# One more pair of half-products in a fused attention and feed-forward kernel, and a new order of its instructions

## The chip, the cores and the metric

The kernel runs on one core of a Trainium2 chip. The metric is the device time of one execution in microseconds (us). Besides the core's engines TensorE (PE; its weight loads are PEld), VectorE (DVE), ScalarE (ACT) and GpSimd (POOL), the queue of SyncE (SP) issues the transfers (DMA).

## The reference

Three stages follow each other, with B = 2 sequences of 448 tokens, 12 heads of 64 and a model width of 768:

```python
attn = softmax(where(causal, q @ k.T / 8, -1e9)) @ v          # per head
x = attn as [896 tokens, 768]
h = maximum(maximum(x @ w1, x @ w2), x @ w3)                  # 768 x 768 each
y = h @ w_out                                                 # 768 x 768
g = where(z > 0, z, exp(minimum(z, 0)) - 1), z = y @ w_in     # 768 x 2048
out = g @ w_out2                                              # 2048 x 768
```

All of it is in float32.

## The kernel before, in words

**Products.** A matrix product of float32 accuracy is made of three matmuls: both factors are split into a high and a low part in the type fp32r, and hi*hi, hi*lo and lo*hi are summed in PSUM. A block is one 128-column block f of a weight matrix, for both sequences; its moving operand is 128 x 448. `standard` makes one block of ph (x times w1, w2 or w3; n = 0, 1, 2) with 2 x 6 x 3 = 36 matmuls of 448 columns. `unit` makes two blocks at once in the manner of Strassen: seven half-products of 9 matmuls each, 63 in all, where two standard blocks need 72. Its operands are the two blocks' weights and differences of them (f13, f24), and, of x, sums that are made once for all units (`sums_x`).

**Weights.** A weight block comes by DMA as raw int64 and goes through `load_steps`: three short DVE steps (L184, L187, L189), one ACT step (L191), one DVE step (L193); then ACT makes hi (L211, L727 in a unit) and DVE makes lo (L199). A unit adds one difference of full width and two halves (L744) and takes four splits to hi and lo instead of two. What a block's matmuls leave in PSUM goes to SBUF through ACT for n = 0 (L233) and is joined by DVE with a maximum for n = 1 and 2 (L235); in a unit two of the four outputs first get the shared term s5 added by DVE (L628). During a unit ACT copies the running sum from one PSUM bank to another three times (L799) and s5 once (L813).

**Stages.** The attention of 12 head pairs comes first (until 93.3 us on PE); scores `s`, transposes `pt` of the probabilities and outputs `o` alternate there, and 54 matmuls of early ph blocks fill gaps. ACT or DVE copies a transposed bank from PSUM to SBUF (`th<-pt`, L271) before PE may reuse it; there are two banks. Then come ph, py = h times w_out, pg (with the exp) and po, where three pairs of pg and two of po are units too (the last is o4). In ph block 0, block 5 and, of n = 0, the blocks 1 and 2 are standard; units are made of the block pairs (1, 2) and (3, 4): 1_1, 2_1, 0_3, 1_3, 2_3 (n, first block).

**Order.** Every engine works its instructions off in the order written. That order comes from a planner, `Plan`: a list of tasks with costs per engine (ns), needs, buffers taken and given, and a rank; at each step it takes the task that can begin first, or one within `SLACK` ns of that with a smaller rank. One plan covers the attention (its ranks are `LEADS` and `SHIFTS`, and the engine of a normalise, a guard or a copy is chosen by it), one, `late_plan`, all the rest (ranks are PE's time at the task). `LAG` is the time from a task's end to its follower's start. Nothing of these numbers runs on the chip: they decide order and, where a task may go to several engines, the engine.

Of the kernel before, what the change touches and what calls it, by code (L numbers as in the profile page):

```python
# [51 lines left out]
    "exps": -18.87, "guard": -543.14, "inverse": -213.22, "keep": 263.11, "least": 284.28, "load": -700.35,  # L52
# [4 lines left out]
    "x_hi": -414.57, "x_lo": -284.77,  # L57
}
SHIFTS = {
# [10 lines left out]
class Plan:  # L70
# [9 lines left out]
    SLACK = 62  # L80
# [5 lines left out]
    SWITCHES = 100  # L86

# [5 lines left out]
    def add(self, fn, args, engines, pair, after=(), takes=(), gives=(), mode=None, lead=None):  # L93
        if lead is None:
            lead = LEADS.get(f"{fn.__name__}{args[0]}" if args else None, LEADS.get(fn.__name__))
        rank = pair + lead + self.shifts.get(len(self.tasks), 0)
        t = {"fn": fn, "args": args, "engines": engines, "pair": pair, "rank": (rank, len(self.tasks)),
             "after": [a for a in after if a], "takes": list(takes), "gives": list(gives), "mode": mode}
        self.tasks.append(t)
        return t  # L100
# [4 lines left out]
    def begins(self, t, free):  # L105
        ready = {}
        for e, cost in t["engines"].items():
            at = free[e] + (self.switch(t["mode"]) if e == "PE" else 0)
            for a in t["after"]:
                at = max(at, a["end"] + (35 * (e in self.OVER) if a["eng"] == e else self.LAG[a["eng"]]))  # L110
            for k in set(t["takes"]):
                n = t["takes"].count(k)
                if len(self.slots[k]) < n:
                    return None
                at = max(at, sorted(self.slots[k])[n - 1])
            ready[e] = at
        return min((at + t["engines"][e], at, e) for e, at in ready.items())

    def order(self, free=()):
        free = dict.fromkeys(self.LAG, 0) | dict(free)  # L120
        left, out = list(self.tasks), []
        while left:
# [8 lines left out]
            free[eng] = end - self.OVER.get(eng, 0)  # L131
            if eng == "PE":
                self.mode = t["mode"]
# [15 lines left out]
def fused_kernel(ctx: ExitStack, tc: tile.TileContext, qk, v, w1, w2, w3, wo, wi2, wo2, outT):  # L149
# [93 lines left out]
    with ExitStack() as s2:  # L243
# [58 lines left out]
        def add_totals(c, k, after=None, plan=plan, lead=20):  # L302

            t1, t2, t3, t4 = (totals[q, c] for q in range(4))
            out, a, b = ((t3, t2, t1), (t2, t1, t2), (t4, t4, t2))[k]

            def total(eng):
                nc.vector.tensor_tensor(out=out, in0=a, in1=b, op=ALU.subtract)

            need = [kept[c], kept[NPAIR + c]] if k == 0 else [after]  # L310
            return plan.add(total, (), {"DVE": 619}, 0, need, lead=NPAIR + c + THIRD if k == 0 else lead + c)

        def pair(p):
# [142 lines left out]
            def finish(s):  # L456
# [3 lines left out]
                for part in PARTS:  # L460
# [3 lines left out]
                    for i, j in sorted(mine, key=lambda ij: -ij[0]):  # L464
                        w = min(C * (i + 1), S)
                        flat[i, j] = plan.add(
                            normalise, (i, j), {"POOL": 240 + int(0.84 * w), "DVE": 100 + int(0.7 * w)}, p, [a])
# [36 lines left out]
        def weights(k):  # L504
# [8 lines left out]
            for s, (eng, cost) in enumerate((("DMA", 4200), *LOAD[1:], ("ACT", 760), ("DVE", 880))):  # L513
                t = plan.add(
                    step, (), {eng: cost}, GATES[k], [t or xs_done[GATES[k]]], takes={0: ["raw"], 1: ["f"]}.get(s, []),
                    gives={5: ["raw"], 7: ["f"]}.get(s, []))
# [32 lines left out]
        for steps in begun.values():  # L549
# [5 lines left out]
            for k, (eng, cost) in enumerate(LOAD):  # L555
                t = plan.add(
                    step, (), {eng: cost}, B * NPAIR, [t or xs_done[NPAIR + HALF + 1], xs_done[NPAIR + HALF + 2 - (k == 0)]],
                    takes=[["raw"], ["f"]][k] if k < 2 else [], gives=["raw"] * (k == len(LOAD) - 1), lead=19)
# [24 lines left out]
    late_plan.OVER = {"DVE": 60, "ACT": 60}  # L583
    late_plan.SLACK = 110
    late_plan.LAG = Plan.LAG | {"ACT": 120, "DVE": 120}
# [111 lines left out]
    def unit(name, src, lean, left, sums, leave, kind="p"):  # L697
# [74 lines left out]
        split("13", tk, "t", at + 1800, [t1, opened], slice(0, NK), [(ut, name, 2)])  # L772
        split("24", tk, "t", at + 3600, [t4, opened], slice(0, NK), [(u, name, 3)] if lean else [ut])
# [59 lines left out]
    for f in UNITS[0]:  # L833
        standard(0, f, range(B))
# [13 lines left out]
    for fs_ in UNITS:  # L848
        for n in range(1 if fs_ == UNITS[0] else 0, 3):
# [188 lines left out]
    if PO_UNITS:  # L1038
        for c in range(HALF):
            d, tot, t = c + HALF, {}, None  # L1040
            at = begin + 22000 + 6000 * c
# [23 lines left out]
    def put(f, b, ps, after, at, eng, gives, more=None, frees=()):  # L1065
# [11 lines left out]
        task(lambda eng: None, "-", 2500, at, [t], gives=["ot"])  # L1077
# [82 lines left out]
```

## Time and profile before

| | |
|---|---|
| runs, us | 474.38, 476.13, 1632.58; median 476.13 |
| profiled execution, us | 475.4, of which the span is 473.5 |
| busy: PE, DVE, ACT, POOL | 464.2, 397.7, 281.4, 46.5 us |
| granted clock of PE over the span | 0.999 |
| attention on PE | to 93.3 us |
| ph after the attention, py | 93.3 to 203.6, from 203.6 us |

The profiled execution lies 0.7 us below the median; 1.9 us of it lie outside the span. In the rows below a time is us from the start of the span; a duration behind the start is that of the instruction (a group "x2" that of both), and the number in brackets is the idle time of the engine before it, with the instruction that ended it. PE's matmuls are pipelined: one starts before the one ahead has ended, so its pace is read from starts.

### The profile page before, as it was taken

To read this page: it belongs to the slowest core of one execution; us is meant where nothing else is said; L and a number is where in the kernel's file an instruction comes from. 1 tells how busy PE (TensorE), PEld (TensorE's weight loads), DVE (VectorE), ACT (ScalarE), POOL (GpSimd) and SP (SyncE) were. 2 spreads that over 40 slices of the span, in tenths; PEclk is the share of its full clock that TensorE was granted. 3 is DMA by queue.
4 is the path that set the end of the run, shared out by engine and by line. 5 is a ranking of instruction groups with operands and counts; after the bars stand their busy time and mean duration, and the time that the engine had idled before them with its cause. 6 is when DMAs were issued, how large, how long until landed. Compare 5 with 4: busy or idle time off the path is not lost.

```text
span 473.5 us, 6942 instructions
## 1 busy us (share of the span) xinstructions
PE 464.2 (98%) x2510; PEld 408.1 (86%) x2510; DVE 397.7 (84%) x826; ACT 281.4 (59%) x574; POOL 46.5 (10%) x97
## 2 busy tenths in 40 slices
PE   8999989999999999999999999999999999999997
PEld 3665757799999999999999999999999999999896
DVE  4999998499899999899989898999879999677301
ACT  6999885492455655454645887888766435433300
POOL 3655673000000000000000000000000000000000
PEclk9999999999999999999999999999999999999999
DMA  6652422223435234323331331434343431655002
GB/s 210 213 168 112 138 74 65 93 78 124 157 117 190 70 134 135 127 82 125 134 133 68 115 122 38 143 118 133 125 122 112 141 118 63 184 173 177 13 0 78
DMA packets 13969, 55.88 MB, mean 118 GB/s; under 512 B 1520, under 2 KB 3568, under 8 KB 13936
## 3 DMA queue, kind: packets, MB, share of 16 engines
q1 hardware_dynamic: 13936, 55.45, 35.0%
q8 instruction: 19, 0.31, 0.3%
q14 instruction: 14, 0.11, 0.1%
HBM read 52.69 MB, written 2.75 MB: 117 GB/s over the span
## 4 chain that ended last, share of the span: by engine, by line
PE 80%; DVE 10%; DMA 4%; ACT 2%; POOL 2%; issue 1%; SPq 0%; DVEq 0%; ACTq 0%; POOLq 0%
PE pg L895 10%; PE p L786 8%; PE py L895 6%; PE ps L786 6%; PE po L895 5%; PE pg L899 5%; PE ph L222 4%; PE ph L224 4%; PE ph L221 4%; PE pg00g L786 3%; PE pt L386 3%; PE py L899 3%; DMA raw_wo<-in_wo 3%; PE po L899 3%; PE s L339 3%; PE o L409 2%
## 5 line engine op out<-in xcount | busy, mean ns | idle before, releaser
L895 PE MATMUL pg<-x,hi_wi 128*128 128x448 f32 x240 | 57.7, 362 | 0.0
L895 PEld LDWEIGHTS pg<-x,hi_wi 128*128 128x128 f32 x240 | 45.0, 188 | 3.0
L363 ACT ACTIVATE pr<-pr,nmx 128x384 f32<-128x384 f32 (+2 forms) x72 | 35.9, 503 | 6.3 <-DVE nmx L353 5.8
L221 PE MATMUL ph<-x,hi_w 128*128 128x448 f32 x96 | 36.2, 377 | 0.0
L222 PE MATMUL ph<-x,hi_w 128*128 128x448 f32 x96 | 35.0, 364 | 0.1
L895 PE MATMUL py<-h,hi_wo 128*128 128x448 f32 x144 | 34.6, 362 | 0.0
L376 POOL TENSOR_SCALAR pr<-pr,r 128x256 f32<-128x256 f32 (+2 forms) x62 | 32.4, 541 | 21.0 <-DVE r L372 10.7
L899 PE MATMUL pg<-x,lo_wi 128*128 128x448 f32 x120 | 33.7, 362 | 0.0
L353 DVE CUSTOM_DVE_ANT_0 pr<-s,mask 128x384 f32<-128x384 f32 (+2 forms) x72 | 26.3, 414 | 6.0 <-PE s L339 6.0
L191 ACT ACTIVATE f_wo<-f_wo,lift 128x640 uint32<-128x640 int16 (+1 forms) x20 | 17.3, 873 | 21.4 <-DVE f_wo L189 21.4
L224 PE MATMUL ph<-x,lo_w 128*128 128x448 f32 x96 | 30.0, 363 | 0.0
L895 PEld LDWEIGHTS py<-h,hi_wo 128*128 128x128 f32 x144 | 27.0, 188 | 1.8
L339 PE MATMUL s<-qk 64*128 64x384 f32 (+3 forms) x192 | 26.8, 440 | 1.6 <-DMA qk<-in_qk 1.2
L386 PE MATMUL pt<-ident,pr 128*128 128x128 f32 x144 | 22.4, 280 | 2.8 <-ACT th L271 1.9
L386 PEld LDWEIGHTS pt<-ident,pr 128*128 128x128 f32 x144 | 16.0, 140 | 9.8 <-ACT th L271 3.7
L199 DVE SCALAR_TENSOR_TENSOR lo_wo<-f_wo,hi_wo 128x640 fp32r<-128x640 f32 (+1 forms) x20 | 17.5, 874 | 7.8 <-ACT hi_wo L211 7.5
L899 PEld LDWEIGHTS pg<-x,lo_wi 128*128 128x128 f32 x120 | 22.5, 188 | 1.5
L339 PEld LDWEIGHTS s<-qk 64*128 64x128 f32 (+1 forms) x192 | 14.2, 174 | 10.5 <-DVE nmx L353 4.3
L211 ACT ACTIVATE hi_wo<-f_wo 128x640 fp32r<-128x640 f32 (+1 forms) x20 | 15.7, 785 | 12.3 <-PE po00o L895 8.4
L409 PE MATMUL o<-th,v 128*64 128x448 f32 (+2 forms) x144 | 21.7, 439 | 0.0
L899 PE MATMUL py<-h,lo_wo 128*128 128x448 f32 x72 | 20.2, 362 | 0.0
L193 DVE SCALAR_TENSOR_TENSOR f_wo<-raw_wo,f_wo 128x640 int32<-128x640 int32 (+1 forms) x20 | 17.3, 875 | 3.2 <-ACT f_wo L191 3.1
(282 smaller groups left out, 1256.3 us busy)
## 6 DMA issues: line engine op xcount, KB each, us to landing
raw_w<-in_w SPq DMA_DIRECT2D x18, 768.0 KB, 4.4
raw_wo<-in_wo SPq DMA_DIRECT2D x12, 768.0 KB, 4.6
raw_wi<-in_wi SPq DMA_DIRECT2D x10, 768.0 KB, 4.3
raw_wo<-in_wo SPq DMA_DIRECT2D x12, 640.0 KB, 4.2
qk<-in_qk SPq DMA_DIRECT2D x11, 448.0 KB, 4.2
raw_wg<-in_wi SPq DMA_DIRECT2D x6, 768.0 KB, 4.5
v<-in_v SPq DMA_DIRECT2D x12, 256.0 KB, 2.7
out_t<-ot SPq DMA_DIRECT2D x12, 224.0 KB, 2.0
```

What stands on the lines that cost most here:

```text
L221: nc.tensor.matmul(ps, hi[:, c, :], xs[cc][:, 0, :], start=(cc == 0), stop=False)
L222: nc.tensor.matmul(ps, hi[:, c, :], xs[cc][:, 1, :], start=False, stop=False)
L224: nc.tensor.matmul(ps, lo[:, c, :], xs[cc][:, 0, :], start=False, stop=(cc == total - 1))
L339: nc.tensor.matmul(out, us[e]["qk"][own, 0, C * i:w], us[e]["qk"][own, 1, :w], start=True, stop=True, skip_group_check=True)
L353: nc.vector.tensor_tensor_reduce(out=pr, in0=u["s", g][j or 0][:, at:at + w], in1=mask_r if i == NB else mask[:, FULL - w:], scale=-0.125, ...
L363: nc.scalar.activation(pr, pr, AF.Exp, bias=u["nmx"][:, n:n + 1], scale=-1.0, accum_out=u["l"][:, n:n + 1])
L376: engines[eng].tensor_scalar(out=u["pr", j, i], in0=u["pr", j, i], scalar1=u["r"][:, n:n + 1], scalar2=1.0, op0=ALU.mult, op1=ALU.mult)
L386: nc.tensor.transpose(pt[:e - C * c, at:at + C], u["pr", j if j is None else j ^ odd, i][:, C * c:e], ident)
L409: nc.tensor.matmul(u["o"][D * j:D * (j + 1), C * c:], u["v"][:, j, c], u["th_r"][:, j ^ odd] if c == NB else u["th"][:, c, j ^ odd, C * c: ...
L786: nc.tensor.matmul(ps[0], wt[:, HALF * kk + c], w[:, i, :], start=(new and c == m == 0), stop=(c == HALF - 1 and m == 2), skip_group_check ...
L895: nc.tensor.matmul(p[0], hi[:, c, :], xs[j][c0 + c][:, i, :], start=first and c == 0 and i == 0, stop=False, skip_group_check=True)
L899: nc.tensor.matmul(p[0], lo[:, c, :], xs[j][c0 + c][:, 0, :], start=False, stop=last and c == n - 1, skip_group_check=True)
```

## The change

It does four things. The blocks 1 and 2 of n = 0 become a sixth unit, 0_1, ahead of 1_1. The attention's plan knows a port that DVE and POOL share in three kinds of task, costs the steps on DVE, ACT and POOL 3% more, has a larger SLACK and new ranks; so the order within the attention is another one, and some tasks change engine. The late plan assumes that a DMA takes 1000 ns longer to be seen, and lets DVE's steps overlap by 10 ns more. In units the splits "13" and "24" are due 1.2 us earlier, and the sums for po's units are due later for c = 0 by 6 us, for c = 1 by 4 and for c = 2 by 2.

```diff
 LEADS = {
-    "exps": -18.87, "guard": -543.14, "inverse": -213.22, "keep": 263.11, "least": 284.28, "load": -700.35,
+    "exps": 52.55, "guard": -472.28, "inverse": -311.74, "keep": 224.45, "least": 404.69, "load": -635.7,
...
 SHIFTS = {
-    20: 7.26, 22: -5.68, 24: -1.5, 34: -2.97, 62: 2.91, 91: -7.56, 93: -2.32, 96: -3.16, 97: -13.83, 98: -6,
+    22: -0.83, 31: 1.23, 96: -3.49, 97: -11.46, 103: -1.13, 112: 2.49, 119: -0.88, 142: -0.54, 143: -0.44, 176: 8.48,
...
-    SLACK = 62
+    SLACK = 78
...
+    PORT = ("DVE", "POOL")
+    PACE = 1.03
...
+        engines = {e: int(c * self.PACE + 0.5) if e in ("DVE", "ACT", "POOL") else c for e, c in engines.items()}
...
+            if t["port"] and e in self.PORT:
+                at = max(at, free["port"])
...
+            if t["port"] and eng in self.PORT:
+                free["port"] = end
...
-            return plan.add(total, (), {"DVE": 619}, 0, need, lead=NPAIR + c + THIRD if k == 0 else lead + c)
+            return plan.add(
+                total, (), {"DVE": 619}, 0, need, lead=NPAIR + c + THIRD if k == 0 else lead + c, port=True)
...
-                            normalise, (i, j), {"POOL": 240 + int(0.84 * w), "DVE": 100 + int(0.7 * w)}, p, [a])
+                            normalise, (i, j), {"POOL": 240 + int(0.84 * w), "DVE": 100 + int(0.7 * w)}, p, [a], port=True)
...
-    late_plan.OVER = {"DVE": 60, "ACT": 60}
+    late_plan.OVER = {"DVE": 70, "ACT": 60}
+    late_plan.PACE = 1
     late_plan.SLACK = 110
-    late_plan.LAG = Plan.LAG | {"ACT": 120, "DVE": 120}
+    late_plan.LAG = Plan.LAG | {"ACT": 120, "DVE": 120, "DMA": 3000}
...
-        split("13", tk, "t", at + 1800, [t1, opened], slice(0, NK), [(ut, name, 2)])
-        split("24", tk, "t", at + 3600, [t4, opened], slice(0, NK), [(u, name, 3)] if lean else [ut])
+        split("13", tk, "t", at + 600, [t1, opened], slice(0, NK), [(ut, name, 2)])
+        split("24", tk, "t", at + 2400, [t4, opened], slice(0, NK), [(u, name, 3)] if lean else [ut])
...
-    for f in UNITS[0]:
-        standard(0, f, range(B))
...
-        for n in range(1 if fs_ == UNITS[0] else 0, 3):
+        for n in range(3):
...
-            at = begin + 22000 + 6000 * c
+            at = begin + 28000 + 4000 * c
...
-        task(lambda eng: None, "-", 2500, at, [t], gives=["ot"])
+        task(lambda eng: None, "DMA", 700, at, [t], gives=["ot"])
```

The changed kernel is nine lines longer, so its line numbers are 8 to 11 higher (L184 to L199 become L192 to L207, L744 becomes L755, L799 becomes L810).

First place: DVE right behind the last low part of `sums_x`. Before, two standard loads stand there (f_w0_1 and f_w0_2), with the maxima of block 5 (best0_5, best1_5) between:

```order
L184 TENSOR_SCALAR f_w0_1_1620<-raw_w0_1_1554 128x768
L187 TENSOR_SCALAR f_w0_1_1620<-f_w0_1_1620 128x768
L189 TENSOR_TENSOR f_w0_1_1620<-f_w0_1_1620 128x768
L184 TENSOR_SCALAR f_w0_2_1635<-raw_w0_2_1563 128x768
L187 TENSOR_SCALAR f_w0_2_1635<-f_w0_2_1635 128x768
L189 TENSOR_TENSOR f_w0_2_1635<-f_w0_2_1635 128x768
L193 SCALAR_TENSOR_TENSOR f_w0_1_1620<-raw_w0_1_1554,f_w0_1_1620 128x768
L235 TENSOR_TENSOR best0_5_1611<-ph1_0_5_1572,best0_5_1611 128x448
L235 TENSOR_TENSOR best1_5_1614<-ph1_1_5_1573,best1_5_1614 128x448
L199 SCALAR_TENSOR_TENSOR lo_w0_1_1681<-f_w0_1_1620,hi_w0_1_1680 128x768
L193 SCALAR_TENSOR_TENSOR f_w0_2_1635<-raw_w0_2_1563,f_w0_2_1635 128x768
L199 SCALAR_TENSOR_TENSOR lo_w0_2_1690<-f_w0_2_1635,hi_w0_2_1689 128x768
```

With the change the two blocks of unit 0_1 stand there. Ahead of the rows shown, the three short steps stand twice in both kernels, for the same two raw blocks:

```order
L201 SCALAR_TENSOR_TENSOR b_0_1_1620<-raw_w0_1_0_1554,b_0_1_1620 128x768
L243 TENSOR_TENSOR best0_5_1611<-ph1_0_5_1573,best0_5_1611 128x448
L243 TENSOR_TENSOR best1_5_1614<-ph1_1_5_1574,best1_5_1614 128x448
L201 SCALAR_TENSOR_TENSOR b_0_1_1620<-raw_w0_1_1_1563,b_0_1_1620 128x768
L755 TENSOR_TENSOR f13_0_1_1687<-b_0_1_1620 128x768
L207 SCALAR_TENSOR_TENSOR lo0_0_1_1642<-b_0_1_1620,hi0_0_1_1641 128x768
L755 TENSOR_TENSOR f24_0_1_1698<-b_0_1_1620,f13_0_1_1687 128x384
L755 TENSOR_TENSOR f24_0_1_1698<-b_0_1_1620,f24_0_1_1698 128x384
L207 SCALAR_TENSOR_TENSOR lo13_0_1_1696<-f13_0_1_1687,hi13_0_1_1695 128x768
L207 SCALAR_TENSOR_TENSOR lo1_0_1_1690<-b_0_1_1620,hi1_0_1_1689 128x384
L207 SCALAR_TENSOR_TENSOR lo24_0_1_1703<-f24_0_1_1698,hi24_0_1_1702 128x768
```

Behind the same start, DVE now has a full difference, two halves, three full lows and a half low of unit 0_1 (lo0, lo13, lo1, lo24), where there were two lows.

Second place: ACT in the attention, at the first transposes of head pair 9 (th9 from pt9_0, pt9_1, ...; pr10 and pr11 are exps of the pairs 10 and 11, x7 and t0_1 are copies of pair 7's output):

```order
L363 ACTIVATE pr11_0_2_1074,l11_1057<-pr11_0_2_1074,nmx11_1056 128x384
L363 ACTIVATE pr11_0_0_1076,l11_1057<-pr11_0_0_1076,nmx11_1056 128x128
L271 CAST x7_1119<-o7_1078 128x448
L425 COPY t0_1_81<-o7_1078 128x448
L363 ACTIVATE pr11_1_1_1117,l11_1057<-pr11_1_1_1117,nmx11_1056 128x256
L271 COPY th9_1135<-pt9_0_1125 128x384
L271 COPY th9_1135<-pt9_1_1130 128x384
L363 ACTIVATE pr11_0_1_1121,l11_1057<-pr11_0_1_1121,nmx11_1056 128x256
L271 COPY th9_1135<-pt9_3_1144 128x2x128
```

With the change:

```order
L279 CAST x7_1101<-o7_1073 128x448
L434 COPY t0_1_81<-o7_1073 128x448
L372 ACTIVATE pr11_0_2_1063,l11_1053<-pr11_0_2_1063,nmx11_1052 128x384
L372 ACTIVATE pr11_0_0_1065,l11_1053<-pr11_0_0_1065,nmx11_1052 128x128
L372 ACTIVATE pr11_1_1_1118,l11_1053<-pr11_1_1_1118,nmx11_1052 128x256
L279 COPY th9_1132<-pt9_1_1127 128x384
L372 ACTIVATE pr10_None_3_1125,l10_904<-pr10_None_3_1125,nmx10_903 128x448
```

The copy of pt9_0 has left ACT (DVE makes it now), and x7 and t0_1 stand ahead of the exps of pair 11 that they followed.

Third place: ACT in the last unit, o4 (pos0o4, pos1o4 and pos2o4 are the copies of a running sum from bank to bank, s5_o4 the shared term, f_wo2_5_11 a weight step of the last piece):

```order
L799 COPY pos0o4_4542<-po00o4_4510 128x448
L813 COPY s5_o4_4556<-po130o4_4532 128x448
L191 ACTIVATE f_wo2_5_11_4544<-f_wo2_5_11_4544,lift_69 128x640
L799 COPY pos1o4_4569<-po00o4_4510 128x448
L211 ACTIVATE hi_wo2_4_6_4581<-f_wo2_4_6_4500 128x640
L799 COPY pos2o4_4596<-po00o4_4510 128x448
```

With the change:

```order
L810 COPY pos0o4_4548<-po00o4_4516 128x448
L824 COPY s5_o4_4560<-po130o4_4538 128x448
L810 COPY pos1o4_4575<-po00o4_4516 128x448
L199 ACTIVATE f_wo2_5_11_4573<-f_wo2_5_11_4573,lift_69 128x640
L219 ACTIVATE hi_wo2_4_6_4589<-f_wo2_4_6_4509 128x640
L810 COPY pos2o4_4603<-po00o4_4516 128x448
```

The copy pos1o4 now stands ahead of the weight step f_wo2_5_11, which it followed.

## Rows read from the trace of the kernel before

**Rows 1.** The page's part 1: busy time, share, instructions.

```profile
PE 464.2 (98%) x2510; PEld 408.1 (86%) x2510; DVE 397.7 (84%) x826; ACT 281.4 (59%) x574; POOL 46.5 (10%) x97
```

**Rows 2.** Waits of PE, whole run: total us, times, longest.

```profile
PE pt L386 <- ACT th L271: 1.9, 2, 1.2
...
PE pt L386 <- DVE th L271: 0.7, 2, 0.4
PE po00o L786 <- ACT pos1o L799: 0.5, 1, 0.5
```

**Rows 3.** Windows, 100 to 200 us: busy by engine, clock.

```profile
100.00:200.00 100.00, 100.00 (x501) 93.84 (x500) 93.51 (x154) 53.59 (x83) 0.00 (x0) 1.00 0.36 125
```

**Rows 4.** Timeline, PE: start, duration, instruction, idle before.

```profile
94.60 0.36 PE L221 MATMUL ph<-x,hi_w 128*128 128x448 f32 x1
95.10 0.47 PE L222 MATMUL ph<-x,hi_w 128*128 128x448 f32 x1
...
140.60 0.56 PE L786 MATMUL p<-x,hi 128*128 128x448 f32 x2
...
191.00 0.36 PE L786 MATMUL p<-x,hi 128*128 128x448 f32 x1
...
438.60 0.36 PE L786 MATMUL pos0o<-h,lo_o 128*128 128x448 f32 x1
439.46 0.47 PE L786 MATMUL po00o<-x,hi_o 128*128 128x448 f32 x1 [0.50 <-ACT pos1o L799]
...
469.73 0.36 PE L899 MATMUL pos2o<-c,lo_wo 128*128 128x448 f32 x1
```

**Rows 5.** DVE's instructions by line and shape, 118 to 203 us.

```profile
L193 DVE SCALAR_TENSOR_TENSOR b<-raw_w,b 128x768 int32<-128x768 int32 x10 | 9.5, 954 | 1.1 <-ACT b L191 0.7
L199 DVE SCALAR_TENSOR_TENSOR lo<-f,hi 128x768 fp32r<-128x768 f32 x10 | 9.3, 952 | 0.1
...
L189 DVE TENSOR_TENSOR b<-b 128x768 int16<-128x768 int16 x10 | 5.6, 557 | 0.3
L744 DVE TENSOR_TENSOR f<-b,f 128x384 f32<-128x384 f32 x10 | 5.6, 557 | 0.3
L184 DVE TENSOR_SCALAR b<-raw_w 128x768 bf16<-128x768 bf16 x10 | 5.5, 553 | 0.0
L744 DVE TENSOR_TENSOR f<-b 128x768 f32<-128x768 f32 x5 | 4.8, 958 | 0.2
...
L187 DVE TENSOR_SCALAR b<-b 128x768 int16<-128x768 int16 x10 | 3.6, 356 | 0.2
L199 DVE SCALAR_TENSOR_TENSOR lo<-b,hi 128x384 fp32r<-128x384 f32 x5 | 2.8, 551 | 0.0
L628 DVE TENSOR_TENSOR p<-p,s 128x448 f32<-128x448 f32 x4 | 2.5, 631 | 0.2 <-ACT ps L799 0.2
```

**Rows 6.** Timeline, DVE: lo of the first and of the last unit.

```profile
130.67 0.95 DVE L199 SCALAR_TENSOR_TENSOR lo<-b,hi 128x768 fp32r<-128x768 f32 x1
...
183.68 0.95 DVE L199 SCALAR_TENSOR_TENSOR lo<-b,hi 128x768 fp32r<-128x768 f32 x1
```

**Rows 7.** Timeline, DVE and then ACT, before the wait at 439.46.

```profile
436.67 0.50 DVE L184 TENSOR_SCALAR f_wo<-raw_wo 128x640 bf16<-128x640 bf16 x1 [2.45 <-DMA raw_wo<-in_wo]
...
438.15 0.83 ACT L191 ACTIVATE f_wo<-f_wo,lift 128x640 uint32<-128x640 int16 x1 [2.21 <-DVE f_wo L189]
438.88 0.52 ACT L799 COPY pos1o<-po00o 128x448 f32<-128x448 f32 x1
```

**Rows 8.** Timeline, ACT and then PE, at pair 9's first transposes.

```profile
70.45 0.46 ACT L271 COPY th<-pt 128x384 f32<-128x384 f32 x1
...
70.96 0.44 PE L386 MATMUL pt<-ident,pr 128*128 128x128 f32 x2 [1.20 <-ACT th L271]
```

**Rows 9.** Timeline, POOL and then DVE, in pair 10's normalising.

```profile
66.64 3.52 POOL L376 TENSOR_SCALAR pr<-pr,r 128x384 f32<-128x384 f32 x6 [0.44 <-DVE r L372]
...
67.67 0.63 DVE L187 TENSOR_SCALAR f_w<-f_w 128x768 int16<-128x768 int16 x1
```

More of the change, by code (lines that the diff above doesn't have):

```diff
@@ L51 @@
 LEADS = {
-    "exps": -18.87, "guard": -543.14, "inverse": -213.22, "keep": 263.11, "least": 284.28, "load": -700.35,
[4 rows of a table removed]
-    "x_hi": -414.57, "x_lo": -284.77,
+    "exps": 52.55, "guard": -472.28, "inverse": -311.74, "keep": 224.45, "least": 404.69, "load": -635.7,
+    "load_v": 396.21, "normalise": 579.04, "product": 387.48, "scores0": 506.37, "scores1": 154.12,
[3 rows of a table added]
+    "whole": -301.71, "x_hi": -404.34, "x_lo": -415.07,
 }
 SHIFTS = {
[3 rows of a table removed]
[4 rows of a table added]
 }
@@ L91, in __init__, with add @@
         self.parts, self.tasks, self.mode = {}, [], None
-    def add(self, fn, args, engines, pair, after=(), takes=(), gives=(), mode=None, lead=None):
+    def add(self, fn, args, engines, pair, after=(), takes=(), gives=(), mode=None, lead=None, port=False):
         if lead is None:
             lead = LEADS.get(f"{fn.__name__}{args[0]}" if args else None, LEADS.get(fn.__name__))
+        engines = {e: int(c * self.PACE + 0.5) if e in ("DVE", "ACT", "POOL") else c for e, c in engines.items()}
         rank = pair + lead + self.shifts.get(len(self.tasks), 0)
         t = {"fn": fn, "args": args, "engines": engines, "pair": pair, "rank": (rank, len(self.tasks)),
-             "after": [a for a in after if a], "takes": list(takes), "gives": list(gives), "mode": mode}
+             "after": [a for a in after if a], "takes": list(takes), "gives": list(gives), "mode": mode, "port": port}
         self.tasks.append(t)
@@ L119, in order @@
     def order(self, free=()):
-        free = dict.fromkeys(self.LAG, 0) | dict(free)
+        free = dict.fromkeys((*self.LAG, "port"), 0) | dict(free)
         left, out = list(self.tasks), []
@@ L515, in weights @@
                     step, (), {eng: cost}, GATES[k], [t or xs_done[GATES[k]]], takes={0: ["raw"], 1: ["f"]}.get(s, []),
-                    gives={5: ["raw"], 7: ["f"]}.get(s, []))
+                    gives={5: ["raw"], 7: ["f"]}.get(s, []), port=True)
             return t
@@ L557, in fused_kernel @@
                     step, (), {eng: cost}, B * NPAIR, [t or xs_done[NPAIR + HALF + 1], xs_done[NPAIR + HALF + 2 - (k == 0)]],
-                    takes=[["raw"], ["f"]][k] if k < 2 else [], gives=["raw"] * (k == len(LOAD) - 1), lead=19)
+                    takes=[["raw"], ["f"]][k] if k < 2 else [], gives=["raw"] * (k == len(LOAD) - 1), lead=19,
+                    port=True)
         with tc.manual_schedule():
```

12 rows, old and new, of tables (LEADS, SHIFTS) are left out of this document.

## The prediction

> **What bounds the kernel now.** I read the page's busy times first: PE is busy for 464.2 of 473.5 us [rows 1]. Then the waits of PE: apart from waits at the start, little is left, 2.6 us on copies of transposed banks in the attention (1.9 behind ACT, 0.7 behind DVE) and one wait of 0.5 us near the end [rows 2]. Then a window of ph: from 100 to 200 us PE is busy without a gap, at a granted clock of 1.00 (the 2.4 GHz level), while DVE is at 93.5% and POOL does nothing [rows 3]. So the time is the number of matmuls times their pace, plus a few waits; and DVE is the engine that could become the next bound.
>
> The pace is read from starts. Between 140.60 and 438.60 every 448-column matmul starts 0.200 us behind the one ahead: 298.0 us are 1,490 steps of 0.200 [rows 4]. Behind the wait at 439.46 it is slower: 147 matmuls (27 of the unit, 120 of the last pieces) have 146 steps, 29.2 us at 0.200, but the last starts 30.27 us later, so 0.207 a step and 1.1 us lost. The wait at 95.10 (0.50 us from the start ahead, so 0.30 late) left no such trace, as the pace behind it shows [rows 4]. Why one wait changes the pace and another doesn't, no row says; I keep both possibilities.
>
> **PE's work.** Two standard blocks have 72 matmuls, the unit that takes their place 63. Nine fewer, at 0.200: **-1.8 us**, all on the path, since PE has no gap there.
>
> **DVE's work for it.** A standard block's load costs, by [rows 5], 553 + 356 + 557 + 954 + 952 = 3,372 ns, two of them 6.7 us. Their outputs, of n = 0, leave by ACT. The unit costs 2 x (553 + 356 + 557 + 954) = 4,840 for both raw blocks, 958 + 2 x 557 = 2,072 for the differences, 3 x 952 + 551 = 3,407 for the lows and 2 x 631 = 1,262 for adding s5: 11.6 us. DVE has 4.8 us more, and PE passes the stretch 1.8 us sooner. ACT gets some 2.4 us more (at 53.6% busy in this stretch [rows 3] it hides that); transfers are the same two blocks.
>
> What covers it is DVE's lead over PE. Before, the first unit's lo is done at 130.67 + 0.95 = 131.6 and PE starts the unit at 140.60, 9.0 us later; for the last unit it is 184.6 against 191.00, 6.4 us [rows 4, 6]. Taking 4.8 + 1.8 = 6.6 from these leaves 2.4 and -0.2 us, if none of DVE's idle time (6.5 of the 100 us [rows 3]) is won back. The first of all, 0_1, is no problem: from the last low part of the sums, near 115, DVE needs its two loads, two maxima (2 x 0.63) and one low, 7.1 us, so 122; PE comes at 140.6 - 14.4 = 126.2. The later splits of a unit (13, 24) are due earlier in DVE's order than before, which helps the half-products that use them second and third. So the worst places are the units 0_3, 1_3 and 2_3, where I expect leads near zero, and waits of PE between 0 (idle time is won back) and 1.5 us (it isn't, and a split comes after its half-product's turn). I take **+0.5**. What is late next is w_out's first block, for which DVE has the same 6.6 us less; but PE loses there only what DVE has not caught up by then, and these waits themselves give DVE its lead back.
>
> **The last unit.** In the row of ACT the copy pos1o4 stands behind a weight step that waits for DVE, which had waited 2.45 us for a transfer: landing near 436.7, DVE's steps, ACT at 438.15, the copy at 438.88, PE at 439.46 [rows 7, 4]. In the new order the copy stands first and needs only PE's own sum, done before. The weight step that now waits behind it is of a piece used 87 matmuls, some 18 us, later. So the wait goes: **-0.5**. With no wait there, the pace should stay at 0.200: **-1.1** more. The bounds of this second part are 0 (the slower pace comes from something else at the end) and 1.1; I take all, since the unit's own matmuls ran at 0.200 until the wait.
>
> **The attention.** Its work is the same, in another order; what the order can win is PE's waits, 2.6 us, and some time in switching between kinds of matmul. The longest, 1.20 us at 70.96, is for ACT's copies of pair 9's banks, which start at 70.45 behind the exps of pair 11 [rows 8]. In the new order the first of these copies has gone to DVE, so it no longer stands in that queue; the second still stands behind three exps. The other wait behind ACT, the remaining 0.7, is behind pair 10's copies, whose neighbours stand in the same order as before. I take half of the 1.2 and nothing else, about **-0.7** with the smaller ones. Bounds: -2.6 (all waits go), and +2.6 (as many new ones come: on ACT and DVE 65 to 80 instructions stand ahead of each pair's output, in another sequence, and nothing in the trace excludes a new collision).
>
> Four guards, short steps, also go from POOL to DVE, where no wait of PE hangs on them alone, and the port's model keeps weight steps and normalises apart. The row shows what there is to win: L187, 356 ns alone, took 630 ns beside a run of POOL's normalises [rows 9, 5], so 0.27 us of DVE for one instruction. The Trainium skill, "SBUF — State Buffer", section "Who interferes with whom", says that the port pair is an exclusive lock and that the one who loses "fully blocks": by that rule a step behind one normalise would wait for all of it, 3.52 / 6 = 0.59 us [rows 9]. The trace has 0.27, less than a whole one. With ten such steps the order could free at most 3 us of DVE by the row and 6 by the rule; both are DVE's, and PE gains no more of them than the 2.6 us of waits.
>
> **The sum.** 475.4 - 1.8 + 0.5 - 0.5 - 1.1 - 0.7 = **471.8 us** against the profiled execution, which lies 0.7 below the median shown.
>
> **Rivals.**
> 1. DVE becomes the bound in the last three units. For it: 93.5% busy with 4.8 us to add and 1.8 us less time makes 98.3 of 98.2 us; DVE would have to run without a gap, and 1.1 us of its gaps were waits for ACT's step inside a load [rows 3, 5]. Against: the leads start at 6 to 9 us. Then PE waits for what isn't won back, 2 to 4 us in place of 0.5: 473.3 to 475.3, the whole gain of the unit eaten. Chance 0.15.
> 2. The other side: one such wait, at 0_3 (PE near 164), changes the pace to 0.207 as the wait at 439.46 did. From there some 1,500 matmuls follow; 1,500 x 0.0073 = 11 us, and the 1.1 of the end isn't won: 471.8 + 11 = 483, slower than before. It decides from the first wait on that the pace doesn't forget. For it: 147 matmuls kept it to the end. Against: the wait at 95.10 left none, and it needs a wait first. From 0_1 on (126 us) it would be 1,690 x 0.0073 = 12 us, 484. Chance 0.11.
> 3. The attention's new order is worse: new waits of 2.6 us instead of 0.7 won, so 475.1; twice that gives 478. For it: the planner's model is not the chip. Against: the one wait that can be followed by its queue gets shorter. Chance 0.13.
> 4. The wait at the end stays or comes elsewhere in po, since the loads of the last pieces are also moved (both transfers now stand behind four outputs on SP's queue) and the sums of po's units are due later: -1.8 + 0.5 - 0.7 alone, 473.4. Chance 0.10.
> 5. The attention wins all its 2.6 and the units lose nothing: 475.4 - 1.8 - 1.6 - 2.6 = 469.4. Chance 0.12.
>
> The forecast itself, 470 to 474, has 0.39.
>
> **Range and chances.** The forecast, the rivals 1, 3, 4 and 5 lie between 469 and 478.5; left out are rival 2 and what I don't see. So 468.5 to 478.5. Two per cent, about what a measurement of this kernel can tell from no change, are 9.5 us: faster is below 466.6, slower above 485.7. No case reaches 466.6: 0.03 for what I don't see. The pace of rival 2 with rival 3's waits would pass 485.7: 0.03. Within 2%: 0.94.
>
> **What would show it.** Right: 63 matmuls in place of 72 at a pace of 0.200; PE's waits on DVE's lo in the units under 1.5 us in sum; no wait on pos1o4 and 0.200 to the end; py begins near 201 to 202 (203.6 - 1.8 + 0.5 - 0.7 = 201.6). Wrong: starts 0.207 apart behind the first wait (rival 2); waits of PE for lo of 2_3 or of w_out over 2 us (rival 1); PE leaving the attention later than 93.3 (rival 3).

## The result and the profile after

The changed kernel takes 471.38 us (median of 4 runs, 470.25 to 471.69), the kernel before in the same series 475.65: a ratio of 0.9914, 95% interval 0.9886 to 0.9942. It is a little faster, and inside the 2% called no change. The forecast was 471.8. An execution over 1.5% above the fastest of its kernel (1632.58 us of the kernel before, and one of 482.17 and one of 483.92 further down) counts in a median and not in a ratio. Without the 1632.58 the kernel before has a median of 475.17, and in the later series, to which the ratios of the experiments refer, 475.02 to 475.44.

The profiled execution took 470.25 us, its span is 468.4: 5.1 less than the 473.5 of before. That is more than the 4.3 between the medians (3.8 from 475.17), because the profiled execution of the changed kernel is the fastest of its four, 1.1 us below their median. The page's first part, answering [rows 1]:

```profile
PE 461.6 (99%) x2501; PEld 406.8 (87%) x2501; DVE 400.7 (86%) x833; ACT 287.0 (61%) x582; POOL 44.0 (9%) x93
```

Nine matmuls fewer, 3.0 us more of DVE, 5.6 more of ACT. The waits of PE (us in total, times, longest; two more at the start are left out), answering [rows 2]:

```profile
PE s L348 <- DMA qk<-in_qk: 1.4, 2, 1.0
...
PE pt L395 <- POOL pr_None L385: 0.2, 1, 0.2
PE pt L395 <- DVE th L279: 0.2, 1, 0.2
```

The reader is to see what is missing: no wait on ACT is left, in the attention or at the end, and none on a `lo` of the units. The window from 100 to 200 us, answering [rows 3] (duration of the window, then busy time of PE, PEld, DVE, ACT, POOL, the granted clock):

```profile
100.00:200.00 100.00, 100.00 (x502) 93.88 (x501) 96.71 (x160) 54.83 (x86) 0.00 (x0) 1.00 0.34 120
```

DVE went from 93.5 to 96.7 and PE still has no gap. PE's timeline at the borders of the stages (first ph behind the attention, py, po, the last matmul), answering [rows 4]:

```profile
91.75 0.47 PE L229 MATMUL ph<-x,hi_w 128*128 128x448 f32 x1
...
200.26 0.36 PE L904 MATMUL py<-h,hi_wo 128*128 128x448 f32 x1
...
353.26 0.36 PE L904 MATMUL po<-h,hi_wo 128*128 128x448 f32 x1
...
464.66 0.36 PE L908 MATMUL pos2o<-c,lo_wo 128*128 128x448 f32 x1
```

One border of the kernel before is needed beside those of its rows and its table, the start of po:

```profile
356.60 0.36 PE L895 MATMUL po<-h,hi_wo 128*128 128x448 f32 x1
```

Cut at these borders the difference falls apart into clean parts. The same cuts serve for every experiment; the first transpose (pt) separates the start, which waits for the first transfers, from the attention. The cuts are of the profiled execution, the median is of all:

| kernel | start to pt | pt to ph | ph to py | py to po | po to last | median us |
|---|---|---|---|---|---|---|
| before | 11.87 | 81.43 | 110.30 | 153.00 | 113.13 | 475.65 |
| changed | 12.65 | 79.10 | 108.51 | 153.00 | 111.40 | 471.38 |
| unit alone, first series | 12.33 | 81.35 | 109.70 | 158.10 | 115.11 | 482.01 |
| unit alone, again | 12.81 | 81.41 | 109.17 | 153.00 | 111.55 | 473.67 |
| unit and earlier splits | 12.01 | 81.37 | 108.51 | 153.00 | 111.40 | 472.22 |
| lag of a DMA alone | 14.21 | 81.43 | 110.31 | 153.00 | 111.40 | 474.76 |
| changed, no unit | 12.73 | 79.50 | 110.31 | 153.00 | 111.40 | 472.57 |
| changed, old attention | 12.32 | 81.55 | 108.51 | 153.00 | 111.40 | 472.35 |
| changed, no port | 14.27 | 81.03 | 109.13 | 153.00 | 111.40 | 473.06 |
| changed, late splits | 13.19 | 79.48 | 109.11 | 158.10 | 115.11 | 480.38 |
| changed, a wait early | 13.00 | 79.08 | 109.87 | 153.00 | 111.40 | 472.91 |
| changed, DVE late in 1_3 | 12.54 | 79.54 | 109.01 | 153.00 | 111.40 | 471.44 |
| unit alone, a wait in pg | 14.20 | 81.41 | 109.17 | 154.39 | 111.40 | 476.12 |
| changed, one more pair in pg | 12.93 | 79.08 | 108.51 | 151.90 | 113.08 | 471.61 |

The difference is +0.78 at the start, -2.33 in the attention, -1.79 in ph, 0 in py and pg, -1.73 in po: -5.07. The start differs from profile to profile (11.87 to 14.27 in these fourteen) with the landing of the first transfers; nothing is read from it. The attention takes 79.08 to 79.54 in the six profiles with the whole of the new order and 81.35 to 81.55 in the seven with the old one, so its gain is 1.8 to 2.5.

### The profile page after: what moved, and what is told of

It reads as the page before. It is cut to its first block, busy times and chain, and to the rows that moved or that the text cites. A ratio compares the mean times of both kernels' runs of the same rounds, so it can differ in the third digit from the quotient of the medians.

```text
span 468.4 us, 6919 instructions
## 1 busy us (share of the span) xinstructions
PE 461.6 (99%) x2501; PEld 406.8 (87%) x2501; DVE 400.7 (86%) x833; ACT 287.0 (61%) x582; POOL 44.0 (9%) x93
## 4 chain that ended last, share of the span: by engine, by line
PE 93%; DVE 3%; DMA 1%; POOL 1%; ACT 1%; issue 0%; SPq 0%
PE pg L904 10%; PE p L797 9%; PE ps L797 7%; PE py L904 6%; PE po L904 5%; PE pg L908 5%; PE pt L395 4%; PE s L348 4%; PE o L418 4%; PE pg00g L797 3%; PE py L908 3%; PE ph L230 3%; PE ph L232 3%; PE ph L229 3%; PE po L908 3%; PE po00o L797 2%
## 5 line engine op out<-in xcount | busy, mean ns | idle before, releaser
L385 POOL TENSOR_SCALAR pr<-pr,r 128x384 f32<-128x384 f32 (+2 forms) x62 | 32.3, 540 | 22.4 <-DVE r L381 15.5
L199 ACT ACTIVATE f_wo<-f_wo,lift 128x640 uint32<-128x640 int16 (+1 forms) x20 | 17.4, 875 | 19.0 <-DVE f_wo L197 19.0
L229 PE MATMUL ph<-x,hi_w 128*128 128x448 f32 x72 | 27.4, 381 | 0.0
L230 PE MATMUL ph<-x,hi_w 128*128 128x448 f32 x72 | 26.2, 365 | 0.1
L207 DVE SCALAR_TENSOR_TENSOR lo_wo<-f_wo,hi_wo 128x640 fp32r<-128x640 f32 (+1 forms) x20 | 17.5, 875 | 7.5 <-ACT hi_wo L219 7.2
L232 PE MATMUL ph<-x,lo_w 128*128 128x448 f32 x72 | 23.2, 363 | 0.0
L797 PE MATMUL ps<-x,hi 128*128 128x448 f32 x72 | 20.2, 362 | 0.0
L797 PE MATMUL p<-s,hi 128*128 128x448 f32 x72 | 20.2, 362 | 0.0
```

The source lines that it names most:

```text
L229: nc.tensor.matmul(ps, hi[:, c, :], xs[cc][:, 0, :], start=(cc == 0), stop=False)
L230: nc.tensor.matmul(ps, hi[:, c, :], xs[cc][:, 1, :], start=False, stop=False)
L232: nc.tensor.matmul(ps, lo[:, c, :], xs[cc][:, 0, :], start=False, stop=(cc == total - 1))
L385: engines[eng].tensor_scalar(out=u["pr", j, i], in0=u["pr", j, i], scalar1=u["r"][:, n:n + 1], scalar2=1.0, op0=ALU.mult, op1=ALU.mult)
L797: nc.tensor.matmul(ps[0], wt[:, HALF * kk + c], w[:, i, :], start=(new and c == m == 0), stop=(c == HALF - 1 and m == 2), skip_group_check ...
```

## Experiments: does each part bring its own time?

**The unit alone.** The kernel before, with this edit and nothing else:

```diff
-    for f in UNITS[0]:
-        standard(0, f, range(B))
...
-        for n in range(1 if fs_ == UNITS[0] else 0, 3):
+        for n in range(3):
```

> The kernel before with the sixth unit alone: old tables, old port-free plan, old due times of the splits, old order at the end. Theory (the gains are three separate ones): PE leaves the attention at 93.3 us as before, py begins at 203.6 - 1.8 = 201.8, the wait of 0.5 us on pos1o4 and the slower pace behind it stay: span 473.5 - 1.8 = 471.7 us. Rival (DVE becomes the bound without the earlier splits): PE waits for a lo of the units 0_3, 1_3 or 2_3, 0.3 to 1.5 us in sum, and py begins at 202.1 to 203.3. Rival (one such wait changes the pace): 0.207 from there on, span near 482.

Measured: 482.01 us, ratio 1.014, interval 1.0125 to 1.0155: slower than before by 1.4%, inside the 2% called no change but clear of the noise, and all four executions lie between 481.84 and 482.35. This is the second rival of the prediction, which ended at 483. PE's timeline in unit 1_3 shows where:

```profile
179.19 0.56 PE L786 MATMUL p<-s,hi 128*128 128x448 f32 x2
179.59 0.40 PE L786 MATMUL p<-s,lo 128*128 128x448 f32 x1
179.83 0.56 PE L786 MATMUL p<-s,hi 128*128 128x448 f32 x2
180.23 0.37 PE L786 MATMUL p<-s,lo 128*128 128x448 f32 x1
180.44 0.57 PE L786 MATMUL p<-s,hi 128*128 128x448 f32 x2
...
181.06 0.57 PE L786 MATMUL p<-s,hi 128*128 128x448 f32 x2
...
476.59 0.36 PE L897 MATMUL pos2o<-c,lo_wo 128*128 128x448 f32 x1
```

DVE's timeline just before, and that of the weight loads (PEld), show why:

```profile
177.98 0.62 DVE L628 TENSOR_TENSOR best<-ps,s 128x448 f32<-128x448 f32 x1
178.51 0.95 DVE L199 SCALAR_TENSOR_TENSOR lo<-f,hi 128x768 fp32r<-128x768 f32 x1
```

```profile
179.51 0.19 PEld L786 LDWEIGHTS p<-s,lo 128*128 128x128 f32 x1
```

Up to 179.59 three matmuls take 0.60 us. The lo13 of the unit is done at 178.51 + 0.95 = 179.46, just too late for its weight load, because an addition (L628) stands ahead of it: the load starts at 179.51, 0.08 ahead of its matmul, where the loads around it start 0.20 ahead of theirs. The step from 179.59 to 179.83 is 0.24 instead of 0.20. From there three take 0.61 or 0.62 (179.83, 180.44, 181.06), and they do so to the end: py to po took 158.10 instead of 153.00 (765 matmuls, 0.2067 each), po 115.11 instead of 111.40. No list of waits names this: PE was never idle long enough to count, and the granted clock is 1.00 throughout. Late weights in 0_3, 0.15 to 0.11 us each, had not changed the pace.

**Changed kernel, no unit.** The two lines of the first diff put back into the changed kernel.

> The changed kernel with the blocks 1 and 2 of n = 0 standard again; all orders else by the new numbers. Theory of separate gains: attention until 91.75 us, py at 200.26 + 1.8 = 202.06, no wait at the end, span 468.4 + 1.8 = 470.2 us. Rival (the order's gains hang on the unit): the wait on pos1o4 or new waits in the attention come back, span 471.5 to 473.

Measured: 472.57 us, ratio 0.9944 (0.9929 to 0.9959), span 470.7. The cuts give 110.31 in ph as before, and all other gains stay: the unit brings 1.80 on its own, and the orders do not depend on it.

**Changed kernel, old attention.** The old `LEADS`, `SHIFTS`, `SLACK = 62`, `PORT = ()`, `PACE = 1`.

> The changed kernel with the attention planned by the old ranks, SLACK 62, no port and no pace. Theory of separate gains: PE leaves the attention at 93.3 us instead of 91.75, py begins at 201.8, the rest is unchanged: span 468.4 + 1.55 = 469.95 us. Rival (an earlier end of the attention is given back by DVE, which starts the unit's loads at the same time anyway): PE waits less in the units and the span is 468.4 to 469.2.

Measured: 472.35 us, ratio 0.9936 (0.9921 to 0.9951), span 470.6. The attention takes 81.55 instead of 79.10, and nothing behind it moves: DVE gives nothing back.

By the medians these two steps are smaller: 472.57 and 472.35 lie 1.2 and 1.0 us above the changed kernel's 471.38, where the cuts give 1.8 and 2.4, and the intervals of the three ratios overlap. So the sizes of the parts rest on the cuts; the medians agree in direction alone.

**The lag of a DMA alone.** In the kernel before:

```diff
-    late_plan.LAG = Plan.LAG | {"ACT": 120, "DVE": 120}
+    late_plan.LAG = Plan.LAG | {"ACT": 120, "DVE": 120, "DMA": 3000}
```

> The kernel before with the late plan's lag of a DMA at 3000 alone, by which the copy pos1o4 stands ahead of the weight step f_wo2_5_11 on ACT. Theory (the wait sets the slower pace behind it): the wait of 0.5 us goes and the pace is 0.200 to the end, span 473.5 - 0.5 - 1.1 = 471.9 us. Rival (the slower pace belongs to the end of the program): only the wait goes, the pace of the last 147 matmuls is 0.207, span 473.0 us.

Measured: 474.76 us against 475.31, ratio 0.9983 (0.9972 to 0.9994); its profile, with a slow start, 474.1 of span. The cut from po to the last matmul is 111.40 instead of 113.13, so both the wait and the slower pace behind it are gone in that execution. ACT's timeline there:

```profile
439.55 0.52 ACT L799 COPY pos1o<-po00o 128x448 f32<-128x448 f32 x1 [1.26 <-PE po00o L786]
441.85 0.84 ACT L191 ACTIVATE f_wo<-f_wo,lift 128x640 uint32<-128x640 int16 x1 [1.78 <-DVE f_wo L189]
```

And that of the changed kernel:

```profile
433.86 0.52 ACT L810 COPY pos1o<-po00o 128x448 f32<-128x448 f32 x1 [1.27 <-PE po00o L797]
436.02 0.83 ACT L199 ACTIVATE f_wo<-f_wo,lift 128x640 uint32<-128x640 int16 x1 [1.65 <-DVE f_wo L197]
```

In both the copy waits for PE alone and runs two microseconds ahead of the weight step that it stood behind in [rows 7]. Over the runs the edit brings 0.55 us in the medians, not 1.73. So the profiled execution of before probably had the end worse than most, which no second profile of that kernel shows. With the same old order on ACT the unit alone, repeated, reached the end with 111.55, and the run with earlier splits with 111.40. In these DVE starts on the transferred piece 2.45 and 2.10 us behind ACT's copy pos0o4, in the kernel before 3.07: the transfer landed earlier against PE. The new order takes the dependence on that transfer away; in these profiles that is worth 0 to 1.7 us. The 10 ns of overlap and the later sums for po were not run by themselves.

## Experiments: the lead of DVE and the pace of PE

**A wait behind ACT, early.** In `seed` of the changed kernel, for the first copy of unit 0_1:

```diff
-                nc.scalar.copy(to[0], ps[0])
+                for _ in range(EXTRA if name == "0_1" and to is b else 1):    # EXTRA = 5
+                    nc.scalar.copy(to[0], ps[0])
```

> The changed kernel in which ACT writes the first bank-to-bank copy of unit 0_1 five times instead of once (same values), so that PE waits for it once, by about 0.8 us, near 128 us. If a wait can set the slower pace, and this one does: 0.207 a matmul from there to the end, some 1,690 x 0.0067 = 11 us, span 468.4 + 0.8 + 11 = 480. If the pace stays at 0.200: only the wait, span 469.2 us.

Measured: 472.91 us (471.90 to 474.68), span 470.1. PE waited 1.06 us, ph took 1.36 us longer, and the pace stayed at 0.200 to the end (153.00 and 111.40). A long wait need not turn the pace.

**DVE 0.87 us later in unit 1_3.** In `less_of` of the changed kernel:

```diff
+                for _ in range(2 if what == "13" and name == "1_3" else 1):
+                    nc.vector.tensor_tensor(out=out, in0=a, in1=b, op=ALU.subtract)
-                nc.vector.tensor_tensor(out=out, in0=a, in1=b, op=ALU.subtract)
```

> The changed kernel in which DVE writes the difference f13 of unit 1_3 twice (same values), 0.87 us more work. The trace of the changed kernel has lo13 of that unit 0.27 us ahead of its use. Theory (the unit left DVE no lead there): PE waits some 0.6 us at 177 us. Then either the pace stays, span 469.0, or it turns to 0.207 for the 1,440 matmuls behind, 9.6 us, span 478.6. Rival (there is more lead than the starts show, since PE takes weights late): no wait, span 468.4.

Measured: 471.44 us, ratio 0.9909 (0.9874 to 0.9945), span 469.3. PE's timeline at the unit's first and second half-product:

```profile
175.39 0.56 PE L798 MATMUL p<-x,hi 128*128 128x448 f32 x2
176.04 0.47 PE L798 MATMUL p<-x,lo 128*128 128x448 f32 x1
176.35 0.57 PE L798 MATMUL p<-x,hi 128*128 128x448 f32 x2
...
177.97 0.47 PE L798 MATMUL p<-s,lo 128*128 128x448 f32 x1
178.28 0.57 PE L798 MATMUL p<-s,hi 128*128 128x448 f32 x2
```

The weights lo0 and lo13 come late: starts 0.65 and 0.31 apart where 0.40 and 0.20 are due, and 0.31 again behind 177.97; ph takes 0.50 us longer. So the lead in this unit was below 0.87 us, as its rows say: in the changed kernel lo13 is done at 175.64 + 0.95 = 176.59, and PE begins with that half-product at 176.86. The third matmul, 0.40 us later, is the first that reads lo13, so there is more lead than 0.27, and PE lost 0.50 us in place of the 0.6 expected. DVE's timeline, and PE's, of the changed kernel:

```profile
175.64 0.95 DVE L207 SCALAR_TENSOR_TENSOR lo<-f,hi 128x768 fp32r<-128x768 f32 x1
176.51 0.62 DVE L639 TENSOR_TENSOR best<-ps,s 128x448 f32<-128x448 f32 x1
...
190.06 0.95 DVE L207 SCALAR_TENSOR_TENSOR lo<-f,hi 128x768 fp32r<-128x768 f32 x1
```

```profile
176.86 0.56 PE L797 MATMUL p<-s,hi 128*128 128x448 f32 x2
...
191.26 0.56 PE L797 MATMUL p<-s,hi 128*128 128x448 f32 x2
```

Here lo13 stands ahead of the addition (L639) that it followed in the unit alone; the last rows are lo24 of unit 2_3 and its half-product. With DVE late the pace stayed at 0.200.

**The unit and earlier splits.** The kernel before with the first diff and

```diff
-        split("13", tk, "t", at + 1800, ...
+        split("13", tk, "t", at + 600, ...
-        split("24", tk, "t", at + 3600, ...
+        split("24", tk, "t", at + 2400, ...
```

> The kernel before with the sixth unit and the splits 13 and 24 due 1.2 us earlier, all else old. Theory (in the run with the unit alone, lo13 of unit 1_3 came a tenth of a microsecond late behind an addition of DVE, and that wait set the slower pace): now lo13 stands ahead of that addition, no late weight, pace 0.200 until the wait on pos1o4, which stays: span 473.5 - 1.8 = 471.7. Rival (the splits alone do not give the lead; the lag of a DMA does): late weights again in 0_3 to 2_3, and 480 if one turns the pace.

Measured: 472.22 us, ratio 0.9934 (0.9901 to 0.9967), span 470.1. From ph to py it takes 108.51, to the hundredth what the changed kernel takes: no weight is late. It came out 1.6 us under the expectation because the wait on pos1o4 did not come.

**Changed kernel, late splits.** The same lines back to 1800 and 3600 in the changed kernel.

> The changed kernel with the splits 13 and 24 due as late as before (1,800 and 3,600 behind the unit's time). Theory (the earlier splits are what covers the sixth unit): in the units 0_3, 1_3 and 2_3 an addition of DVE stands ahead of lo13 again, late weights of 0.4 to 0.7 us in sum, py begins that much later, span 468.8 to 469.1; in executions in which a late weight turns the pace, 478 to 480. Rival (the start of the attention's order or the lag of a DMA gives the lead): no late weight, 468.4.

Measured: 480.38 us, ratio 1.0106 (1.0078 to 1.0134), four executions from 479.76 to 480.54. PE's timeline in unit 2_3:

```profile
190.44 0.56 PE L797 MATMUL p<-s,hi 128*128 128x448 f32 x2
190.93 0.47 PE L797 MATMUL p<-s,lo 128*128 128x448 f32 x1
191.24 0.57 PE L797 MATMUL p<-s,hi 128*128 128x448 f32 x2
...
191.86 0.57 PE L797 MATMUL p<-s,hi 128*128 128x448 f32 x2
```

A weight late by 0.03 us at 178.4 left the pace; the one at 190.93, 0.49 behind a pair that takes 0.40, turned it to 0.62 for three (191.24 to 191.86). That weight is lo13, done at 189.93 + 0.95 = 190.88, and the addition (L639) stands ahead of it again:

```profile
188.73 0.62 DVE L639 TENSOR_TENSOR ps<-ps,s 128x448 f32<-128x448 f32 x1
...
189.93 0.95 DVE L207 SCALAR_TENSOR_TENSOR lo<-f,hi 128x768 fp32r<-128x768 f32 x1
```

With the run before this settles which part of the change covers the sixth unit: the earlier splits, in the old plan and in the new one. Without them the steps over 0.200 add up to some 0.25 us of late weights; 9.15 us more, by the cuts, are the pace (5.10 and 3.71 from py on, 0.34 in ph), which a late weight need not turn, as the next two runs show.

**A second wait, late.** The unit alone with five copies (as above) at the first seed of pg's first unit.

> The kernel with the sixth unit alone (480.4 us of span, pace 0.207 from 180 us on), in which ACT also writes the first bank-to-bank copy of pg's first unit five times, so that PE waits about 0.8 us near 265 us. If a wait can also bring the pace back: 0.200 behind it for some 1,030 matmuls, -6.9 us, span 474.3. If the slow pace is kept by something that the program does from there on: span 481.2.

Measured: 476.12 us, ratio 1.0015 (0.9987 to 1.0043). The question was not answered: late weights stand at 168.7 and 181.8 us as in the run of the unit alone, and at 194.3, but here the pace never turned (py to pg 43.21 us for 216 matmuls, 0.200 each; only the wait in pg made py to po longer), so there was no slow pace to bring back. That a program which is the same up to 265 us was slow from 180 on in one run and not in another led to the next.

**The unit alone, again.** The same kernel as in the first experiment.

> The kernel with the sixth unit alone once more, unchanged. In its first run the pace turned to 0.207 behind a weight that came 0.04 us late at 179.8 us (482 us in all its executions); the same program with a longer copy at 265 us had weights late at the same places by nearly the same time and kept 0.200 (474 to 478). If the program decides the pace: slow again from 180 us, 482. If it is not the program but when the weight comes, by some hundredths of a microsecond, which differs from loading to loading: pace 0.200, span 473.5 - 1.8 + some 0.5 of late weights, 472.2, and 474.

Measured: 473.67 us in the median; seven executions from 472.54 to 474.25 and one of 482.17; ratio 0.9965 (0.9944 to 0.9986). PE's timeline at the place that turned the pace in the first run:

```profile
179.74 0.56 PE L786 MATMUL p<-s,hi 128*128 128x448 f32 x2
180.14 0.39 PE L786 MATMUL p<-s,lo 128*128 128x448 f32 x1
180.37 0.57 PE L786 MATMUL p<-s,hi 128*128 128x448 f32 x2
...
180.98 0.56 PE L786 MATMUL p<-s,hi 128*128 128x448 f32 x2
```

The same late weight, 0.23 instead of 0.24 from the second start to the third, then 0.61, and from there 0.200 a matmul (py to po took 153.00). So one program has both paces. What decides between them (the hundredths by which a weight is late, the loading of the program, the chip) stays open. The chip is a rival that no run excludes: the two series in which all four executions were long (the unit alone, late splits) ran on one chip, and the unit alone, again, on another. But the run without the port was on that same chip as well, had a wait of 0.6 us and two late steps (0.03 and 0.07 us) in ph, and kept 0.200 in its profile. The execution of 482.17 was not profiled; only its length speaks for the slower pace. A late weight or a wait goes directly before the slower pace in each profile that shows it (before, the unit alone, late splits), and six other profiles have one and kept 0.200; of the profiles without either, apart from the short wait for x at the first ph (changed, no unit, old attention, lag alone, earlier splits), none shows it. In the unit alone the late weights themselves cost 109.17 - 108.51 = 0.66 us.

**Without the port.** `PORT = ()` in the changed kernel, all else as it is.

> The changed kernel whose attention is planned without the shared port; ranks, SLACK and the 3% as they are. Only the attention differs. If the port's model makes the order good: waits of PE come back, some 1 to 2 us, and weight steps beside POOL's normalises are longer (L195 over 385 ns in the mean); span 469.5 to 470.5. If the ranks alone do it: 468.4, apart from the start.

Measured: 473.06 us in the median (nine executions from 472.06 to 474.39, one of 483.92), ratio 0.9959 (0.9945 to 0.9973). The attention takes 81.03 us instead of 79.10: nearly all of its gain is gone. Ph loses 0.62 us more; its one long wait is for a copy on ACT that stands behind two outputs of h, which had waited for DVE. Its longest waits of PE behind the start (the second is in unit 0_1, the others are in the attention):

```profile
...
PE pt L395 <- ACT th L279: 0.6, 1, 0.6
PE p L797 <- ACT ps L810: 0.6, 1, 0.6
PE pt L395 <- DVE th L279: 0.4, 1, 0.4
PE pt L395 <- POOL pr L385: 0.3, 1, 0.3
...
```

DVE's weight steps in the attention (count, total us and mean ns of one), without the port:

```profile
L192 DVE TENSOR_SCALAR f_w<-raw_w 128x768 bf16<-128x768 bf16 x3 | 2.0, 670 | 0.0
...
L197 DVE TENSOR_TENSOR f_w<-f_w 128x768 int16<-128x768 int16 x3 | 1.9, 617 | 0.1
...
L195 DVE TENSOR_SCALAR f_w<-f_w 128x768 int16<-128x768 int16 x3 | 1.6, 533 | 0.1
```

And in the changed kernel:

```profile
L192 DVE TENSOR_SCALAR f_w<-raw_w 128x768 bf16<-128x768 bf16 x4 | 2.3, 587 | 0.0
...
L197 DVE TENSOR_TENSOR f_w<-f_w 128x768 int16<-128x768 int16 x3 | 2.1, 694 | 0.1
...
L195 DVE TENSOR_SCALAR f_w<-f_w 128x768 int16<-128x768 int16 x4 | 1.5, 385 | 0.1
```

By these means two of the three steps are longer by 83 and 148 ns and one is shorter by 77: half a microsecond over nine steps, in an attention that is 1.9 longer. So the model's use lies in the order more than in shorter steps. It is no proof that a port is what it models: the ranks were kept, and an order made with other rules from the same ranks may be worse for that alone. The ranks, the SLACK and the 3% were not run one by one.

**One more pair, in pg.** `PG_UNITS = (2, 6, 10, 13)` in the changed kernel. It leaves out one thing: the fourth pair's sums of y are not kept, and it reads them from tiles that blocks of g have already taken over. So it doesn't compute the function; it is run to see what DVE's extra work costs in this order, and a version that kept the sums could have another order.

> The changed kernel with a fourth pair of pg in half-products (blocks 13 and 14). PE has nine matmuls less: span 468.4 - 1.8 = 466.6 us if DVE's lead covers it. DVE has 4.8 us more in a stretch of pg and po where it is busy 22.4 to 24.2 of 25 us. Theory (DVE's lead is what a further unit costs): from 325 to 400 us DVE has 5 us free, so the lead shrinks but PE waits little, 0 to 0.5 us: span 466.6 to 467.1. Rival (a late weight turns the pace): 0.207 for the some 560 matmuls behind, +3.8, span 470.4.

Measured: 471.61 us, ratio 0.9926 (0.9907 to 0.9944), span 469.3 beside 468.4. From py to po it takes 151.90 instead of 153.00, so 0.7 of the 1.8 is lost there, and po takes 113.08, 1.68 more. The waits:

```profile
...
PE po130o L797 <- DVE x L166: 0.7, 1, 0.7
PE pg00g L797 <- ACT pgs1g L810: 0.4, 1, 0.4
PE pos2o L797 <- ACT pos2o L810: 0.3, 1, 0.3
```

DVE has no lead left in this stretch: the sums of g that po's first unit needs come late. The pace stayed. No version here beats the changed kernel by more than the noise.

## Why the prediction was right, step by step

**Nine matmuls, -1.8.** Right: -1.79, and 1.80 when the unit is taken out again.

**DVE's lead, +0.5.** The place and the mechanism were right (leads near zero in 0_3 to 2_3; counted to the start of the half-product the smallest are 191.26 - 191.01 = 0.25 us at lo24 of 2_3 and 0.27 at lo13 of 1_3), and the sum of waits was 0, so the term was too dear. DVE's extra work was sized at 4.8 us by adding whole durations, but in the rows a step of DVE often starts some 0.1 us before the one ahead has ended: its busy time grew by 3.1 us (400.7, and 397.6 without the unit). The step treated the earlier splits as a help; the runs show that they are the condition. Without them the late weights cost 0.66 us where the pace kept (the unit alone, again), near the 0.5, and open the way to the slower pace.

**The end, -0.5 and -1.1.** Right for the profile: -1.73. The 0.207 a step contains one longer step right behind the wait (0.31 us); the others are 0.2067. Over the runs the kernel before pays only a part of it.

**The attention, -0.7.** Mis-sized: -2.33, near the bound of -2.6. I took half of the longest wait. In the changed kernel DVE and ACT copy pair 9's banks side by side, as the timelines of the two show,

```profile
70.47 0.55 DVE L279 COPY th<-pt 128x384 f32<-128x384 f32 x1
```

```profile
70.55 0.47 ACT L279 COPY th<-pt 128x384 f32<-128x384 f32 x1
```

and the wait of 1.20 us [rows 8] is gone; that behind ACT of 0.68 is gone too, which I had expected to stay, and of 0.7 behind DVE 0.2 are left. The start took back 0.78, which I had not costed at all. The sum came within 1.5 us of the profile (-3.6 said, -5.1 found), and of the medians (-4.3) within 0.7. That the time came out so near the 471.8 is in part luck: the two terms that were off, by 0.5 and 1.6 us, were off the same way, and the uncosted start and a profile below the median took most of that back.

**The rivals.** The second (a late weight turns the pace, 483) did not happen to the changed kernel but is real: 482.01 and 480.38 in two kernels that differ from it by due times or the plan. Its weak point was "the pace doesn't forget": of nine profiles with a late weight or a wait behind the attention, six kept the faster pace or came back to it. Rival 1 (2 to 4 us of waits) was too dear without the earlier splits already, 0.66. Rivals 3 and 4 did not come. Rival 5 (the attention wins all its waits, the units lose nothing, 469.4) is what the profile shows part by part, but for 0.3 us of the attention; with the start's 0.78 it gives 470.2, and 470.25 was measured. So the forecast's range held, and of its mechanisms the one given 0.12 came nearest.

The rule of the Trainium skill ("SBUF — State Buffer", section "Who interferes with whom"), that the loser at the port fully blocks, is not borne out here as a block of a whole normalise: of the weight steps beside normalises, in the profiles of before, changed and without the port, the most lengthened is one L195 of 675 ns, 319 over the 356 of L187 alone, and one L187 of the kernel before took 338 ns although a normalise of 547 ns had started 0.05 us ahead of it. The profile's times of POOL are rough, and no run here isolates one collision.

## What to carry to other kernels

Before an engine off the critical path is given more work, subtract it from that engine's lead over the bound engine at each place of use, and order what the bound engine reads first ahead of what only empties a buffer: here two due times decided whether weights came late, and late weights cost now under 1 us, now some 9. Cut profiles at the borders of stages; behind the attention the parts without a wait agreed to 0.01 us between kernels, while the executions of one kernel varied by 1 us and more. A wait of hundredths can cost far more than itself, and a list of waits need not show it: compare the starts of like instructions before and behind.

## What the runs showed of the hardware that was not expected

Matmuls of 448 columns ran back to back at 0.2000 or at 0.2067 us, both at a granted clock of 1.00 and each for hundreds of microseconds; the change came behind a weight load that was late by 0.04 to 0.1 us or a wait of 0.5 us. Other such late weights (0.03 to 0.25 us) and waits of 0.3 to 1.1 us left the pace alone, and one program has both: the profile of its second series shows 0.200, that of its first 0.2067. What decides is not known. The Trainium skill, "TensorE: Matmul & The Clock Gate", section "Wait — 56ns, not 53.3ns?", gives for back-to-back matmuls a step of N / 2.4 GHz and about 2.5 ns more. By that an estimate for 448 columns is 189 ns. The runs show two steps, both longer; each matmul here has a weight load of its own, of which that section does not speak.
